# Lightning attention and a tanh-shrink MLP on one core: one quarter-product of the first matmul moved to a second Strassen level

## The chip, the cores and the metric

The kernel runs on 1 core of one Trainium2 chip. The metric is the device time in microseconds (us) of one execution; lower is better. Beside it stands one profiled execution, from which all rows below come.

## The reference, cut to what matters

```python
# q, k, v: (4, 8, 768, 64) float32; lam: (8,); w_in: (512, 2048); w_out: (2048, 512)
# attention with decay, in blocks of 64 tokens; kv_state is carried from block to block
for b in range(nb):
    intra = einsum('bhic,bhjc->bhij', qb, kb) * Dmask      # lam ** (i - j), lower triangle
    out   = einsum('bhij,bhjd->bhid', intra, vb) + einsum('bhid,bhde->bhie', qb * lam_pow, kv_state)
    kv_state = lam_block * kv_state + einsum('bhsd,bhse->bhde', kb * rev_pow, vb)
x = out.transpose(0, 2, 1, 3).reshape(3072, 512)           # tokens x (heads * head_dim)
h = x @ w_in                                               # first product:  3072 x 512 x 2048
g = h - tanh(h)
return g @ w_out                                           # second product: 3072 x 2048 x 512
```

## The kernel before

Tokens are worked in 6 groups `g` of 512 (128 positions of each of the 4 batches; `NG = 6`). The hidden dimension of 2048 is cut into 4 units `u` of 512 (`NU = 4`). For each group the order is: the first product, unit by unit (`up`), then tanh and subtraction, then the second product (`down`), and between these, in small pieces, the attention of the next group (`pieces`).

Both matrix products are Strassen-Winograd products: seven quarter-products P1 to P7 in place of eight, with sums of the operands made before and sums of the results made after. From the third group on (`g >= GI`, `GI = 2`) this is done:

- **First product.** P1 and P5 are made in two levels, for all four units at once: `inner_steps` runs seven steps (`STEPS`), each of four matmuls of 128x128 by 128 columns, one for each unit. Their token sums come from `inner_tokens` at the end of the group before, their weight sums from `inner_weights` in the second group, which also sends three of them to DRAM (`fine_in`). The steps 5, 6 and 3 read such a weight sum back as a piece. P2, P6, P7, P3 and P4 are made in one level by `up(g, u, n)`: four matmuls of 128x128 by 256 columns. `later_units` writes their order out.
- **How a unit is put together.** P1's result lies in the buffer S1 of `hidden`, P5's in buffer 22. `seeded` copies them on ScalarE into a bank of PSUM ahead of a product, which then adds to them: P2 to P1 in bank w; P6, P7 and P4 to P1 in bank ya or yb (even or odd unit); P3 to P5 in bank z. `finish` makes tanh on ScalarE (line 651) and the subtraction on VectorE (line 656). The 12 quarter is what stands after P6 (copied on ScalarE, line 662) plus bank z after P3 (VectorE, line 674). The 22 quarter adds P7 on VectorE (line 665). The 21 quarter is read straight from the bank after P4. `up_sums` (lines 698, 699) makes two operand sums of the second product on VectorE.
- **Second product.** `down_twice` makes its quarter-products in two levels: seven steps of four matmuls (line 935) in the order 1, 2, 6, 5, 7, 3, 4. Steps 1, 6, 7 and 4 add up in one bank, and ScalarE copies what stands there after each (line 938). Each operand has three sums on VectorE (`sums_twice`, line 893) and one between steps 2 and 3. The factors are pieces of 256 KB that GpSimd's queue brings from DRAM into a ring of 7 tiles (`piece`, `RING`); the order is that of `pieces_of`. `PLACES` names the PSUM banks.
- **The cover.** In the last unit, `later_units` makes the sums of the second product's P4 on VectorE and puts the attention piece "P2" of the next group (`att_both`: lines 511, 497, 461, 525 on TensorE; then two copies on ScalarE, line 415), or in the last group `down(g, 1)`, ahead of `up(g, 3, 4)`. Then the second product starts with its P4.

Each engine runs its instructions in the order in which they are recorded. PSUM has eight banks: ya, yb, z and w once each, and four under the name att.

Of the kernel before, what the change touches and what calls it, by code (L numbers as in the profile page):

```python
# [16 lines left out]
AL = mybir.AluOpType  # L17
# [7 lines left out]
def kernel(  # L25
# [188 lines left out]
    SLOT = (1, 2, 3, 6, 5, 7, 4)  # L214
    fine = dram.tile([len(TWICE), len(SUB), 128, NU, 128], F32, name="fine")

    fine_in = dram.tile([2, 3, 128, NU, 128], F32, name="fine_in")
# [409 lines left out]
    def up(g, u, n, wait=False, inside=False):  # L627
# [21 lines left out]
        def finish(c, src):  # L649
            th = work.tile([128, 2, HB], F32, name="th", tag="th")  # L650
            tied(g == 0, nc.scalar.activation(th, src, AF.Tanh))  # L651
            if g >= GI:
                pieces(g, ("t", u, c))
                if (u, c) in ((2, 12), (3, 12), (3, 22)):
                    next(made[g, 2], None)
            tied(g == 0 or g >= GI and inside, nc.vector.tensor_tensor(dst(c), src, th, op=AL.subtract))  # L656

        if g >= GI:
            if n == 2:
                finish(11, t)  # L660
            elif n == 6:
                nc.scalar.activation(dst(12), t, AF.Copy)
            elif n == 7:
                def end():
                    tied(inside, nc.vector.tensor_tensor(dst(22), dst(22), t, op=AL.add))
                    finish(22, dst(22))

                if wait:
                    return end
                end()  # L670
            elif n == 4:
                finish(21, t)
            else:
                tied(inside, nc.vector.tensor_tensor(dst(12), dst(12), t, op=AL.add))  # L674
                finish(12, dst(12))
            return
# [24 lines left out]
    INNER = (1, 5)  # L701
    toks = {}

    def a_quarter(n, u, i, k):
        return w1[u][:, k, 0, ts(i, 128)] if n == 1 else ws[u][:, 0, k, ts(i, 128)]

    def inner_weights(u, ns=INNER):
        for n in ns:
            a11, a12, a21, a22 = (a_quarter(n, u, i, k) for i in range(2) for k in range(2))
            t = late["pool"].tile([128, 4, 128], F32, name="ws2", tag="sums", bufs=4)  # L710
# [4 lines left out]
            nc.gpsimd.dma_start(out=fine_in[INNER.index(n)].rearrange("x p u c -> p u x c")[:, u], in_=t[:, 0:3])  # L715

    def inner_tokens(g):
        for n in INNER:
            x = xt[g][FACT[n][1]]
            b11, b12, b21, b22 = (x[:, k, ts(j, 128)] for k in range(2) for j in range(2))  # L720
            t = late["pool"].tile([128, 4, 128], F32, name="tt2", tag="sums", bufs=4)
            t1, t2, t4 = (t[:, x] for x in range(3))
            for dst, x, y in ((t1, b12, b11), (t2, b22, t1), (b12, b22, b12), (t4, b21, t2)):
                nc.vector.tensor_tensor(dst, x, y, op=AL.subtract)
            toks[g, n] = {1: b11, 2: b21, 3: b22, 4: t4, 5: t1, 6: t2, 7: b12}

    STEPS = (1, 5, 2, 6, 7, 3, 4)

    def inner_steps(g, n, tag):

# [1 line left out]
        out4 = hidden(g, "S1" if n == 1 else 22)  # L732
        c11, c12, c21, c22 = (out4[:, :, i, ts(j, 128)] for i in range(2) for j in range(2))
        for x in STEPS:
            b = toks[g, n][x]
            wb = piece(g, ("in", n), x) if x in (3, 5, 6) else None
            dst = w if x == 2 else z if x in (3, 5) else y
            for u in range(NU):
                a = wb.rearrange("p m c -> p (m c)")[:, ts(u, 128)] if wb is not None else a_quarter(
                    n, u, *{1: (0, 0), 2: (0, 1), 7: (1, 0), 4: (1, 1)}[x])  # L740
                tied(True, nc.tensor.matmul(out=dst[:, ts(u, 128)], lhsT=a, rhs=b, start=x in (1, 2, 5) and u == 0,  # L741
                                            stop=True, skip_group_check=True))
# [29 lines left out]

    def pieces_of(g):
        if g >= GI:
            yield from ((g, ("in", 5), x) for x in STEPS if x in (5, 6, 3))
        for n in order(g):
            yield from ((g, n, x) for x in (SUB if twice(g, n) else range(NU)))
        if g == NG - 1:
# [125 lines left out]
    def sum_third(g, n):  # L904
# [5 lines left out]

    PLACES = {GI - 1: {4: ("w", "yb"), 5: ("att", "w"), 6: ("yb", "z"), 7: ("w", "att"), 3: ("z", "att")},
              NG - 1: {4: ("att", "att"), 7: ("att", "yb"), 5: ("att", "w"), 2: ("yb", "ya"), 6: ("w", "att")}}
    PLACES.update({g: {4: ("att", "att"), 7: ("att", "yb"), 5: ("att", "w"), 1: ("yb", "z"), 2: ("w", "ya"),
                       6: ("z", "att"), 3: ("ya", "att")} for g in range(GI, NG - 1)})

    def down_twice(g, n):
        a11, a12, a21, a22 = quarter(g, n)
        s1, s2 = low.pop((g, n))
        places = PLACES[g][n]
        begins = (1, 2) if places[0] == "att" or (g, n) == (GI - 1, 4) else (2,)  # L920
# [301 lines left out]
    def second_units(g):  # L1222
        for u in range(NU):
            for n in (2, 6, 5, 7, 1, 4, 3):
                if n != 1:
                    up(g, u, n)
                elif u + 1 < NU:
                    up(g, u + 1, 1)
                else:
                    pieces(g, u)  # L1230
                    inner_weights(u, INNER[:1])
                    every(down(g, 1))
                if u < 2 and n == 5:
                    sums_in(u + 2)
            inner_weights(u, INNER if u + 1 < NU else INNER[1:])
            if u + 1 < NU:
                pieces(g, u)

    def later_units(g):
        for n in (1, 2):  # L1240
            made[g, n] = fine_factors(n) if g == GI else iter(())
        for u in range(NU):
            if u < 2:
                next(made[g, u + 1], None)
            for n in ("next", 3, "S", 4) if u == 0 else (6, "next", 7, 3, "S", 4) if u + 1 < NU else (
                    6, 3, 7, "S", "P4", "cover", 4):
                if n == "next":
                    up(g, u + 1, 2, inside=True)
                elif n == "S":
                    up_sums(g, u)  # L1250
                elif n == "P4":
                    sums_twice(g, 4)
                elif n == "cover":
                    if twice(g, 1):
                        pieces(g, "P2")
# [4 lines left out]
            pieces(g, u)  # L1260
            if u == 0:
                every(made[g, 1])
            elif u == NU - 1:
                every(made[g, 2])

    def later_products(g):
        product = down_twice(g, 4)
# [35 lines left out]
    for g in range(1, NG):  # L1303
# [6 lines left out]
        if g == NG - 1:  # L1310
            down_end(g)
            continue
        inner_tokens(g + 1)
# [48 lines left out]
```

## Time and profile before

| what | value |
|---|---|
| median of 3 runs | 653.57 us (650.77 to 654.89) |
| profiled execution | 653.5 us, of which the span from first to last instruction is 651.7 us |
| granted TensorE clock, mean | 0.997 |
| TensorE (PE) busy | 641.0 us, 98% of the span, 5792 matmuls |
| VectorE (DVE) busy | 495.3 us, 76%, 884 instructions |
| ScalarE (ACT) busy | 241.2 us, 37%, 484 instructions |
| GpSimd (POOL) busy | 231.1 us, 35%, 396 instructions |
| DMA | 140.45 MB, mean 216 GB/s |

PE, DVE, ACT and POOL are the engines; PEld is the weight load of TensorE, which overlaps PE. L935 is line 935 of the kernel before. An entry such as `y<-wb,g` gives output and inputs by the program's names. The timeline gives start, duration, engine, line, operation, tiles and shape; what stands in square brackets is the idle time of the engine just before it and what ended that. The ends of matmuls are modelled, so rows of PE overlap a little: the distance of two starts is the better measure.

### The profile page before, as it was taken

The page shows a single profiled execution, that of the slowest core. Times are in us where ns is not written, and L with a number is a line of the kernel's source. Part 1 is how long each engine was busy: PE and PEld are TensorE (multiplying, and loading weights), DVE is VectorE, ACT ScalarE, POOL GpSimd, SP SyncE. Part 2 cuts the span into 40 slices and gives each one's busy share as a digit, 9 for nine tenths or more (in the row PEclk, how much of TensorE's full clock was granted, in tenths as well). Part 3 has the DMA queues.
Part 4 walks back from the last instruction along what each step waited for, and adds up shares of the span by engine and source line. Part 5 has one row for each costly group of instructions (what it writes and reads, how often), then busy time and mean ns, then how long its engine had stood idle before and what let it go on. Part 6 is the DMA issues. An engine that isn't in the chain of part 4 may idle for free.

```text
span 651.7 us, 14766 instructions
## 1 busy us (share of the span) xinstructions
PE 641.0 (98%) x5792; PEld 590.9 (91%) x5792; DVE 495.3 (76%) x884; ACT 241.2 (37%) x484; POOL 231.1 (35%) x396
## 2 busy tenths in 40 slices
PE   8999999999999999999999999999999999999998
PEld 6788888888888999888999988999988999988997
DVE  4897988987877967888868777878777878256583
ACT  3878683513322124442122453122344212444110
POOL 2210248783113554233455100546201456300450
PEclk9999999999999999999899999999999999999999
DMA  9879979999468877999878766778693587610482
GB/s 215 248 196 215 253 243 296 323 324 279 127 160 220 265 238 220 246 284 250 268 238 295 197 140 129 246 238 310 194 188 98 164 289 253 209 41 0 156 289 74
DMA packets 108197, 140.45 MB, mean 216 GB/s; under 512 B 63968, under 2 KB 81504, under 8 KB 108128
## 3 DMA queue, kind: packets, MB, share of 16 engines
q0 software_dynamic: 29840, 97.54, 46.8%
q1 hardware_dynamic: 78144, 41.96, 27.2%
q8 instruction: 46, 0.75, 0.5%
q14 instruction: 23, 0.19, 0.1%
q10 hardware_dynamic: 144, 0.00, 0.0%
HBM read 117.18 MB, written 23.86 MB: 216 GB/s over the span
## 4 chain that ended last, share of the span: by engine, by line
PE 86%; issue 5%; DMA 3%; POOL 2%; DVE 2%; ACT 1%; SPq 1%; POOLq 0%; DVEq 0%; ACTq 0%
PE y L935 16%; PE y L643 15%; PE zw L935 12%; PE acc L1045 7%; PE h L1015 6%; PE z L643 6%; PE w L643 5%; PE y L741 4%; PE z L741 2%; PE y L870 2%; DMA wb<-fine 2%; PE sp L461 2%; PE op L511 2%; PE op L497 1%; PE kv L424 1%
## 5 line engine op out<-in xcount | busy, mean ns | idle before, releaser
L817 POOL DMA_DIRECT2D wb<-fine x217 | 116.8, 539 | 220.5 <-PE y L935 112.5
L935 PE MATMUL y<-wb,g 128*128 128x128 f32 x624 | 81.3, 276 | 0.2 <-DMA wb<-fine 0.2
L938 ACT ACTIVATE q<-y 128x128 f32<-128x128 f32 x108 | 30.0, 278 | 138.4 <-PE y L935 138.4
L935 PEld LDWEIGHTS y<-wb,g 128*128 128x128 f32 x624 | 75.3, 192 | 1.1 <-issue 0.6
L935 PE MATMUL zw<-wb,g 128*128 128x128 f32 x416 | 55.2, 276 | 0.7 <-DMA wb<-fine 0.6
L935 PEld LDWEIGHTS zw<-wb,g 128*128 128x128 f32 x416 | 50.6, 192 | 1.2 <-PE y L935 0.8
L643 PE MATMUL y<-xt,w 128*128 128x256 f32 x200 | 46.9, 380 | 0.0
L651 ACT ACTIVATE th<-g 128x512 f32<-128x512 f32 x42 | 26.5, 631 | 51.9 <-DVE g L674 20.3
L1015 PE MATMUL h<-xt,w 128*128 128x256 f32 x192 | 44.2, 382 | 1.4 <-DVE w L325 1.4
L656 DVE TENSOR_TENSOR g<-g,th 128x512 f32<-128x512 f32 x42 | 29.2, 694 | 17.4 <-ACT th L651 17.2
L643 PEld LDWEIGHTS y<-xt,w 128*128 128x128 f32 x200 | 37.6, 190 | 5.1 <-ACT g L683 0.2
L1015 PEld LDWEIGHTS h<-xt,w 128*128 128x128 f32 x192 | 35.7, 190 | 6.8 <-DVE w L325 1.3
L643 PE MATMUL w<-xt,w 128*128 128x256 f32 x168 | 40.4, 382 | 0.0
L643 PE MATMUL z<-xt,ws 128*128 128x256 f32 x168 | 39.7, 379 | 0.0
L643 PE MATMUL y<-tt,w 128*128 128x256 f32 x160 | 38.1, 381 | 0.0
L643 PE MATMUL y<-tt,ws 128*128 128x256 f32 x160 | 38.1, 380 | 0.0
L643 PEld LDWEIGHTS z<-xt,ws 128*128 128x128 f32 x168 | 31.9, 190 | 4.3
L935 PE MATMUL y<-wb,s 128*128 128x128 f32 x248 | 33.8, 281 | 1.5 <-DMA wb<-fine 1.4
L643 PEld LDWEIGHTS w<-xt,w 128*128 128x128 f32 x168 | 31.0, 190 | 4.5 <-ACT w L614 0.4
L643 PEld LDWEIGHTS y<-tt,w 128*128 128x128 f32 x160 | 30.1, 190 | 4.2
L643 PEld LDWEIGHTS y<-tt,ws 128*128 128x128 f32 x160 | 30.0, 190 | 3.9
L935 PE MATMUL zw<-wb,s 128*128 128x128 f32 x248 | 33.5, 279 | 0.0
(216 smaller groups left out, 1376.2 us busy)
## 6 DMA issues: line engine op xcount, KB each, us to landing
wb<-fine POOLq DMA_DIRECT2D x217, 256.0 KB, 3.9
raw<-in_moe_w_in_dram SPq DMA_DIRECT2D x12, 512.0 KB, 5.2
fine<-f POOLq DMA_DIRECT2D x24, 256.0 KB, 4.8
wb<-fine_in POOLq DMA_DIRECT2D x24, 256.0 KB, 4.2
raw<-in_moe_w_out_dram POOLq DMA_DIRECT2D x10, 512.0 KB, 6.3
q_blk<-in_q_dram SPq DMA_DIRECT2D x32, 128.0 KB, 4.4
k_blk<-in_k_dram SPq DMA_DIRECT2D x32, 128.0 KB, 5.1
wb<-factors POOLq DMA_DIRECT2D x16, 256.0 KB, 4.5
```

The source lines that it names most:

```text
L461: tied(True, nc.tensor.matmul(out=dst, lhsT=keys(p, j, late_), rhs=qt[ts(j, 64), p, rows], start=True, stop=True))
L511: tied(True, nc.tensor.matmul(out=dst(n, p, j)[:, HF:BLK], lhsT=vn[:, 2 * p + j, :], rhs=ss[:, j, p % 2, 1 + p // 2, :], start=first and n ...
L643: tied(g == 0, nc.tensor.matmul(out=t[:, m, :], lhsT=wt[:, kt, ts(m, 128)], rhs=x[:, kt, :], start=first and m == 0 and kt == 0, stop=kt = ...
L651: tied(g == 0, nc.scalar.activation(th, src, AF.Tanh))
L656: tied(g == 0 or g >= GI and inside, nc.vector.tensor_tensor(dst(c), src, th, op=AL.subtract))
L741: tied(True, nc.tensor.matmul(out=dst[:, ts(u, 128)], lhsT=a, rhs=b, start=x in (1, 2, 5) and u == 0, stop=True, skip_group_check=True))
L817: nc.gpsimd.dma_start(out=t.rearrange("p m c -> p (m c)"), in_=fine[TWICE.index(n_), SLOT.index(x_)].rearrange("p u c -> p (u c)"))
L870: nc.tensor.matmul(out=t[:, m, :], lhsT=a[:, u, kt, ts(m, 128)], rhs=wb[:, kt, :], start=first and u == 0 and m == 0 and kt == 0, stop=u = ...
L935: tied(True, nc.tensor.matmul(out=dst, lhsT=a[:, u, :], rhs=wb[:, ts(u, 128)], start=x in begins and u == 0, stop=u == NU - 1, skip_group_ ...
L938: nc.scalar.activation(keep, dst, AF.Copy)
L1015: tied(u == 0 or u == 2 and cs[0] == 11, nc.tensor.matmul(out=hm[c][:, m, :], lhsT=w1[u][:, i, a, ts(m, 128)], rhs=xt[0, t][:, i, :], star ...
L1045: nc.tensor.matmul(out=acc[n][:, r, :], lhsT=a[:, ts(r, 128)], rhs=b, start=kt == 0 and r == 0, stop=kt == KH - 1, skip_group_check=True)
```

## The change

From the third group on, P4 of the first product is made in two levels for all units at once, as P1 and P5 are:

- `up(g, u, 4)` is gone from `later_units`. After P7 of each unit, ScalarE copies the bank (P6+P7 on top of P1) into buffer 21.
- `inner_last` ("U4") comes after the last unit's `up_sums` and ahead of the sums of the second product's P4: seven steps of four matmuls of 128 columns, in the order 1, 5, 6, 2, 7, 3, 4, in the banks ya, w, z and one of att. Three of their results are copied on ScalarE (two of them into other banks, to be added to), four are added to buffer 21 on VectorE.
- `finish_last` comes behind the sums of the second product's P4: one addition of 128x1024 to buffer 21, then four times tanh and subtraction.
- The token sums (`inner_tokens(g, 4)`) are taken one by one at the 11 quarter of the units 1 to 3. The weight sums are made in the second group, in tiles of their own, and go to DRAM on ScalarE's queue. Each group has three more pieces in the ring, between those of P5 and those of the second product.
- The second product's P4 moves to the banks z and yb, its P7 to two banks of att. In the third group the last factor sums (`made[g, 2]`) end ahead of "U4" and no longer behind the last unit.

```diff
     def finish(c, src):
             ...
             if g >= GI:
                 pieces(g, ("t", u, c))
                 ...
+                if c == 11 and u:
+                    steps(made[g, "T4"], 1 + u // 3)
...
             elif n == 7:
                 def end():
+                    nc.scalar.activation(dst(21), t, AF.Copy)
                     tied(inside, nc.vector.tensor_tensor(dst(22), dst(22), t, op=AL.add))
                     finish(22, dst(22))
...
+    LAST = (1, 5, 6, 2, 7, 3, 4)
+    def inner_last(g):
+        y, w, z5, z3 = bank("y3", "ya", 1), bank("w3", "w", 1), bank("z5", "att", 4), bank("z3", "z", 1)
+        r5 = otile("r5")
+        out4 = hidden(g, 21)
+        c11, c12, c21, c22 = (out4[:, :, i, ts(j, 128)] for i in range(2) for j in range(2))
+        for x in LAST:
+            dst = {2: w, 3: z3, 5: z5}.get(x, y)
+            inner_matmuls(g, 4, x, dst, x in (1, 5))
+            if x in (1, 6):
+                nc.scalar.activation(w if x == 1 else z3, y, AF.Copy)
+            elif x == 5:
+                nc.scalar.activation(r5, z5, AF.Copy)
+            else:
+                c = {2: c11, 7: c22, 3: c12, 4: c21}[x]
+                hold(c, c, dst.rearrange("q (u c) -> q u c", u=NU), op=AL.add)
+        return r5
+    def finish_last(g, r5):
+        c = hidden(g, 21)
+        cols = c[:, :, :, ts(1, 128)]
+        hold(cols, cols, r5.rearrange("q (u c) -> q u c", u=NU)[:, :, None, :].to_broadcast([128, NU, 2, 128]), op=AL.add)
+        for u in range(NU):
+            th = work.tile([128, 2, HB], F32, name="th", tag="th")
+            nc.scalar.activation(th, c[:, u], AF.Tanh)
+            hold(c[:, u], c[:, u], th, op=AL.subtract)
...
         if g >= GI:
-            yield from ((g, ("in", 5), x) for x in STEPS if x in (5, 6, 3))
+            yield from ((g, ("in", n), x) for n in (5, 4) for x in STEPS if x in (5, 6, 3))
...
-    PLACES.update({g: {4: ("att", "att"), 7: ("att", "yb"), 5: ("att", "w"), 1: ("yb", "z"), 2: ("w", "ya"),
+    PLACES.update({g: {4: ("z", "yb"), 7: ("att", "att"), 5: ("att", "w"), 1: ("yb", "z"), 2: ("w", "ya"),
...
     def second_units(g):
                     inner_weights(u, INNER[:1])
+                    for v in range(u):
+                        inner_weights(v, INNER[2:])
                     every(down(g, 1))
...
     def later_units(g):
+        made[g, "T4"] = inner_tokens(g, 4)
         for u in range(NU):
             ...
-            for n in ("next", 3, "S", 4) if u == 0 else (6, "next", 7, 3, "S", 4) if u + 1 < NU else (
-                    6, 3, 7, "S", "P4", "cover", 4):
+            for n in ("next", 3, "S") if u == 0 else (6, "next", 7, 3, "S") if u + 1 < NU else (
+                    6, 3, 7, "S", "U4", "P4", "cover"):
                 ...
                 elif n == "S":
                     up_sums(g, u)
+                    if u + 1 == NU:
+                        every(made[g, 2])
+                elif n == "U4":
+                    r5 = inner_last(g)
                 elif n == "P4":
                     sums_twice(g, 4)
+                    finish_last(g, r5)
```

More of the change, by code (lines that the diff above doesn't have):

```diff
@@ L215 @@
     fine = dram.tile([len(TWICE), len(SUB), 128, NU, 128], F32, name="fine")
-    fine_in = dram.tile([2, 3, 128, NU, 128], F32, name="fine_in")
+    fine_in = dram.tile([3, 3, 128, NU, 128], F32, name="fine_in")
     w_in_u = moe_w_in.rearrange("k (u a n) -> k u a n", u=NU, a=2)
@@ L699, in up_sums, with inner_weights @@
         tied(g >= GI, nc.vector.tensor_tensor(c12, c11, c12, op=AL.subtract))
-    INNER = (1, 5)
+    INNER = (1, 5, 4)
     toks = {}
     def a_quarter(n, u, i, k):
-        return w1[u][:, k, 0, ts(i, 128)] if n == 1 else ws[u][:, 0, k, ts(i, 128)]
-    def inner_weights(u, ns=INNER):
+        return (w1[u][:, k, 0] if n == 1 else ws[u][:, 0, k] if n == 5 else w1[u][:, 2 + k, 1])[:, ts(i, 128)]
+    def inner_weights(u, ns=INNER[:2]):
         for n in ns:
             a11, a12, a21, a22 = (a_quarter(n, u, i, k) for i in range(2) for k in range(2))
-            t = late["pool"].tile([128, 4, 128], F32, name="ws2", tag="sums", bufs=4)
+            t = otile("ws4").rearrange("p (x c) -> p x c", x=4) if n == 4 else late["pool"].tile(
+                [128, 4, 128], F32, name="ws2", tag="sums", bufs=4)
             s1, s2, s4 = (t[:, x] for x in range(3))
@@ L714, in inner_weights @@
                 tc.keep_in_program_order(nc.vector.tensor_tensor(dst, x, y, op=op))
[L715 to L725, printed above, removed]
@@ L727, with inner_tokens @@
-    STEPS = (1, 5, 2, 6, 7, 3, 4)
+            eng = nc.scalar if n == 4 else nc.gpsimd
+            eng.dma_start(out=fine_in[INNER.index(n)].rearrange("x p u c -> p u x c")[:, u], in_=t[:, 0:3])
+    def inner_tokens(g, n):
+        x = xt[g][FACT[n][1]]
+        b11, b12, b21, b22 = (x[:, k, ts(j, 128)] for k in range(2) for j in range(2))
+        t = otile("tt4").rearrange("p (x c) -> p x c", x=4) if n == 4 else late["pool"].tile(
+            [128, 4, 128], F32, name="tt2", tag="sums", bufs=4)
+        t1, t2, t4 = (t[:, x] for x in range(3))
+        toks[g, n] = {1: b11, 2: b21, 3: b22, 4: t4, 5: t1, 6: t2, 7: b12}
+        for dst, x, y in ((t1, b12, b11), (t2, b22, t1), (b12, b22, b12), (t4, b21, t2)):
+            tied(n == 4, nc.vector.tensor_tensor(dst, x, y, op=AL.subtract))
+            yield
@@ new lines, with inner_matmuls @@
+    STEPS = (1, 5, 2, 6, 7, 3, 4)
+    def inner_matmuls(g, n, x, dst, begin):
+        b = toks[g, n][x]
+        wb = piece(g, ("in", n), x) if x in (3, 5, 6) else None
+        for u in range(NU):
+            a = wb.rearrange("p m c -> p (m c)")[:, ts(u, 128)] if wb is not None else a_quarter(
+                n, u, *{1: (0, 0), 2: (0, 1), 7: (1, 0), 4: (1, 1)}[x])
+            tied(True, nc.tensor.matmul(out=dst[:, ts(u, 128)], lhsT=a, rhs=b, start=begin and u == 0,
+                                        stop=True, skip_group_check=True))
@@ L729, in inner_steps @@
+    def finish_last(g, r5):
+        c = hidden(g, 21)
+        cols = c[:, :, :, ts(1, 128)]
+        hold(cols, cols, r5.rearrange("q (u c) -> q u c", u=NU)[:, :, None, :].to_broadcast([128, NU, 2, 128]), op=AL.add)
+        for u in range(NU):
+            th = work.tile([128, 2, HB], F32, name="th", tag="th")
+            nc.scalar.activation(th, c[:, u], AF.Tanh)
+            hold(c[:, u], c[:, u], th, op=AL.subtract)
     def inner_steps(g, n, tag):
@@ L734, in inner_steps @@
         for x in STEPS:
-            b = toks[g, n][x]
-            wb = piece(g, ("in", n), x) if x in (3, 5, 6) else None
             dst = w if x == 2 else z if x in (3, 5) else y
[L738 to L742, printed above, removed]
+            inner_matmuls(g, n, x, dst, x in (1, 2, 5))
             d = dst.rearrange("q (u c) -> q u c", u=NU)
@@ L919, in down_twice @@
         places = PLACES[g][n]
-        begins = (1, 2) if places[0] == "att" or (g, n) == (GI - 1, 4) else (2,)
+        begins = (1, 2) if places[0] == "att" or n == 4 else (2,)
         y, zw = (bank(name, t, 4 if t == "att" else 1) for name, t in zip(("y2", "zw"), places))
@@ L1234, in second_units @@
                     sums_in(u + 2)
-            inner_weights(u, INNER if u + 1 < NU else INNER[1:])
+            inner_weights(u, INNER[:2] if u + 1 < NU else INNER[1:])
             if u + 1 < NU:
@@ L1262, in later_units @@
                 every(made[g, 1])
-            elif u == NU - 1:
-                every(made[g, 2])
     def later_products(g):
@@ L1312 @@
             continue
-        inner_tokens(g + 1)
+        for n in INNER[:2]:
+            every(inner_tokens(g + 1, n))
         p3 = down_twice(g, 3)
```

## The prediction

> I call the groups g0 to g5 and the units u0 to u3; the change acts in g2 to g5 and, for the weight sums, in g1.
>
> **What bounds the kernel now.** I read the page first: TensorE is busy nearly throughout.
>
> ```profile
> span 651.7 us, 14766 instructions
> ...
> PE 641.0 (98%) x5792; PEld 590.9 (91%) x5792; DVE 495.3 (76%) x884; ACT 241.2 (37%) x484; POOL 231.1 (35%) x396
> ```
>
> Then the waits of TensorE alone. In the changed groups it waits only for pieces in g2, some 2.2 us with the next line of this kind; for VectorE or ScalarE it doesn't wait there at all.
>
> ```profile
> PE y L935 <- DMA wb<-fine: 1.6, 2, 1.4
> ```
>
> Then busy time by stretches: the units of g3 (373 to 410) and its second product (410 to 456). PE fills both to the last tenth; VectorE has 9 us of idle time in the first.
>
> ```profile
> 373.00:410.00 37.00, 37.00 (x335) 33.00 (x332) 28.15 (x42) 16.24 (x30) 1.07 (x2) 1.00 0.62 132
> 410.00:456.00 46.00, 45.94 (x479) 45.24 (x478) 38.22 (x73) 9.73 (x31) 26.84 (x49) 1.00 0.82 277
> ```
>
> So a shorter TensorE sequence shortens the time only while nobody makes TensorE wait. The chain that ended last prices a matmul (x16 is 8 matmuls and 8 weight loads): 3.45/8 = 0.432 us with 256 columns, 1.79/8 = 0.224 us with 128.
>
> ```profile
> 394.18 3.45 PE y L643 x16
> ...
> 412.38 1.79 PE y L935 x16
> ```
>
> Last, the timeline of g3 in two places. First, from P3 of u2 to P3 of u3:
>
> ```profile
> 392.29 1.89 PE L643 MATMUL z<-xt,ws 128*128 128x256 f32 x8
> 392.49 0.69 DVE L665 TENSOR_TENSOR g<-g,y 128x512 f32<-128x512 f32 x1 [0.25 <-PE y L643]
> 393.10 1.15 DVE L354 STREAM_TRANSPOSE kt<-k_blk 128x512 f32<-128x512 f32 x1
> ...
> 394.06 0.71 DVE L656 TENSOR_TENSOR g<-g,th 128x512 f32<-128x512 f32 x1
> 394.66 0.70 DVE L674 TENSOR_TENSOR g<-g,z 128x512 f32<-128x512 f32 x1
> 395.45 0.63 ACT L651 ACTIVATE th<-g 128x512 f32<-128x512 f32 x1 [1.55 <-DVE g L674]
> 395.99 0.58 ACT L619 ACTIVATE z<-g 128x512 f32<-128x512 f32 x1
> ...
> 397.47 1.89 PE L643 MATMUL z<-xt,ws 128*128 128x256 f32 x8
> ```
>
> Bank z is read by L674, refilled by L619, and only then may P3 of u3 start; between the two P3 TensorE has P4 of u2 and P6 of u3. Second, from the cover to the first steps of the second product:
>
> ```profile
> 401.02 1.15 PE L511 MATMUL op<-ss,v_nat 128*64 128x64 f32 x32
> 405.03 1.99 PE L643 MATMUL y<-tt,w 128*128 128x256 f32 x8
> 405.04 1.08 ACT L415 ACTIVATE xt<-op 128x512 f32<-128x512 f32 x2 [1.60 <-PE op L525]
> 406.86 1.05 PE L935 MATMUL y<-wb,g 128*128 128x128 f32 x8
> 407.95 0.28 ACT L938 ACTIVATE q<-y 128x128 f32<-128x128 f32 x1 [0.23 <-PE y L935]
> 408.65 1.06 PE L935 MATMUL y<-wb,s 128*128 128x128 f32 x8
> ```
>
> The third row's two copies and the fifth row's copy are ScalarE's; the last row (step 6) adds to the bank that the fifth row copied, so it must come behind it.
>
> **The change, part by part.** I follow the order of the changed program's instructions on each engine and put the durations of these rows to it.
>
> *A, matmuls.* Per group 16 x 0.432 = 6.91 us go, 28 x 0.224 = 6.26 come: -0.65, four groups -2.6. The first product's own steps stand at 0.89 to 0.95 us for four, so the bounds are -2.8 and -1.0.
>
> *B, P3 of u3 late.* Without P4 of u2, TensorE is at P3 of u3 1.73 us sooner after P3 of u2. In the rows above the bank was full at 396.57 and the weight load began at 397.26, so 0.7 was spare: short by 1.0. ScalarE now copies the ya or yb bank into buffer 21 after P7, and in the built program the addition of line 665 waits for that copy (0.6), with the whole chain behind it: subtraction, L674, tanh, refill. Short by 1.6. VectorE also loses cover before that: P4 of u0 and u1 took 3.45 us of TensorE, but only 1.4 us of subtractions. Counting its 16 operations at their distance of 0.60 to 0.73 and four transposes at 0.96 from 376.25 on, with the waits for ScalarE, the refill ends at 393.8 where TensorE arrives at 392.2: 1.7 in g3 and g4. In g5, without transposes, the chain alone gives 1.6. In g2 four more subtractions (L893, 2.86 us from 274.34) lie before it, partly in waits: I take 3.0. Sum 8.0; bounds 4.0 (1.0 each, if copy and addition could overlap) and 11.
>
> The Trainium skill ("PSUM — Partial Sum Buffer", section "PSUM bank collisions raise a hardware error") says that two engines, readers too, must not be in the same bank and quadrant at once, and that a dependency is put between them. By that rule the copy and line 665 run one after the other, as I have it; without it the sum would be 2.2 lower, 665.3. No row of before has two readers of one bank side by side, so this trace doesn't show it.
>
> *C, waits inside the new product.* Step 7 waits for a ScalarE copy of the same bank, step 4 for VectorE's addition of step 7. VectorE has still to do line 698 and 699 of u3, then the additions of the steps 2 and 7: in g3 these end 0.25 us after TensorE has come to step 4, and 0.1 goes at step 7. Taken: 0.4, 0.4, 0.5 and 0.4, sum 1.7; bounds 0 and 3.2.
>
> *D, step 6 of the second product's P4 late.* From the last matmul of "U4": 0.3 to its result; addition and three sums of P4, 2.55; the addition of 128x1024, 1.2 (line 839's rows); tanh 0.65, subtraction 0.7, and as `th` has two tiles the third tanh waits for the first subtraction and the fourth for the second, 1.25 more: 6.65. On ScalarE, behind these four tanh, stand the two copies of line 415 (1.1) and then the copy that step 6 waits for (0.3): 8.05. TensorE's cover is the attention piece (401.02 to 405.03, 4.0) and the steps 1 and 2 (1.8): 5.8. It waits 2.3 in each of g2, g3, g4: 6.9. In g5 the cover is `down(g, 1)` with 6.9, and line 415 isn't there: 0. Bounds per group 1.8 (every operation at its shortest distance) and 3.0: 5.4 and 9. Nothing later suffers: the fourth sum that step 3 needs comes 1.6 after step 6 has begun, step 3 2.7 after it.
>
> The Trainium skill ("TensorE: Matmul & The Clock Gate", section "Architectural detail: the array is 16× 32×32, not 1× 128×128") says that ScalarE's and VectorE's queues are strictly first in, first out, while TensorE may pull weight loads forward. If a ready copy could pass a waiting tanh, this term would be gone and the sum would give 660.6. The trace agrees with the rule: the refill at 395.99 needed only bank z, free at 395.36, and stood behind the tanh of 395.45.
>
> *E, what is hidden.* The 16 operations for the weight sums of g1 (0.20 apart at line 714: 3.2 us) lie beside `down(1, 1)` (6.9 us), their four DMAs on ScalarE's queue too; without that cover 2 us: bounds 0 and 2. VectorE's twelve small token sums are in B. Three more pieces a group: they take ring places that the second product's P4 had from early on, so its last three pieces are issued during "U4"; the first of them is needed more than 9 us after its issue against a landing of 3.9. In g2 the 2.2 us of waits for pieces may shrink, as TensorE comes later, or grow as GpSimd's queue holds two factor stores behind those pieces: 0, bounds -2.2 and +2. The new banks of P4 and P7 are free before they are wanted (z after the addition of step 3, the att banks after line 415).
>
> **Sum:** -2.6 + 8.0 + 1.7 + 6.9 + 0 = +14.0, against the profiled 653.5 (span 651.7 and 1.8 around it; the median is 0.07 above): **667.5 us**. By group: g2 5.2, g3 and g4 3.7, g5 1.4.
>
> **Rivals.**
> - *Everything hidden.* If the waits of B to D fall into slack that I don't see, A remains: 650.9; with the waits for pieces gone too, 648.7. For it speaks only that 24% of VectorE's and 63% of ScalarE's span is idle; against it, that the waits come from order and not from load. This is the case that ends on the other side. It decides from the point at which bank z is refilled by 392.2 in g3, that is 1.0 sooner after P7 than the rows allow.
> - *Only one of the two waits.* B without C and D: 653.5 - 2.6 + 8.0 = 658.9. D and C without B: 659.5. B is the surer one: it rests on a measured slack of 0.7 against 1.73.
> - *The backlog spreads.* In the second product VectorE is busy for 38.2 of 46 us. If it stays 1 us behind, a step of the next two products waits in g2 to g4 also: 3 x 2 = 6 more, 673.5. Against it: in D TensorE waits longer than VectorE is late.
>
> **Chances.** The forecast 0.64, one wait alone 0.18, all hidden 0.09, spread 0.09. 1% (6.5 us, to 660.1) is about what a measurement of this kernel can tell from no change. Slower by over 1%: nearly all of the forecast, the spread, and a third of the one-wait case (with its terms at their upper bounds): 0.77. Within 1%: the rest, 0.21; faster by over 1% would need more than A and the pieces give: 0.02. All lower bounds together give 658, all upper ones 680. Range 655 to 674: out of it lie the hidden case and the tail of the spread.
>
> **What would show it.** Right: TensorE idle of 1.5 to 3 us ahead of `z<-xt,ws` of u3 once in each of g2 to g5, released by ScalarE (the refill); 2 to 3 us ahead of the third step of the second product's first quarter-product in g2 to g4 and none in g5, released by ScalarE line 976; "U4" at 6.3 to 7 us from first to last step. Wrong: TensorE at 98% or more in these stretches, "U4" much above 7, or waits for `wb` in their place.

## The result, and the profile after

The changed kernel takes 673.78 us (median of 6 runs), the kernel before 653.24 us beside it: ratio 1.0319, 95% interval 1.0290 to 1.0347, so it is slower by 3.2%. The forecast was 667.5 with a range of 655 to 674. The direction was right, the size 6.3 us too small, and the largest single loss lies in a group to which the prediction gave nothing.

The page of the changed kernel, its span and its busy time by engine:

```profile
span 672.0 us, 15039 instructions
...
PE 643.3 (96%) x5888; PEld 591.9 (88%) x5888; DVE 517.0 (77%) x936; ACT 255.3 (38%) x512; POOL 238.1 (35%) x408
```

The profile counts two matmuls for each of the program's, so the 48 more of the change are 96 here. They come to much the same PE time, but PE falls from 98% of the span to 96%. VectorE's and ScalarE's shares grew by one point each; the time went into waits. They are in the list of TensorE's waits (who waits, for whom, us in total, times, the longest):

```profile
PE z L643 <- ACT z L619: 4.2, 4, 1.3
PE y L973 <- ACT q L976: 3.0, 3, 1.8
PE zw L973 <- DVE s L931: 2.1, 1, 2.1
PE y L643 <- ACT g L664: 1.7, 4, 0.7
...
PE y L741 <- DVE g L931: 1.4, 1, 1.4
...
PE zw L973 <- DVE g L931: 1.3, 1, 1.3
PE zw L973 <- issue: 1.3, 1, 1.3
...
PE op L525 <- ACT probe L501: 1.0, 1, 1.0
PE y L908 <- DVE g L931: 0.8, 1, 0.8
```

The first line is term B (P3 of u3 waits until ScalarE has refilled z), the second term D, the fifth term C. The third, sixth and eighth lie in g1; the seventh lies in g2. Only waits of TensorE above 0.2 us are listed, so the sum is a lower bound.

To see where the 20.3 us of longer span arose, I set TensorE's groups of instructions in the two traces side by side and took the growth of the difference of their starts (a group ends here where the units of the next begin):

| group | predicted | measured |
|---|---|---|
| g1 | 0 | 6.8 |
| g2 | 5.2 | 0.9 |
| g3 | 3.7 | 5.4 |
| g4 | 3.7 | 4.0 |
| g5 | 1.4 | 2.8 |

**g1.** The timeline of VectorE in the changed kernel, at the end of the transposes, at the last weight sums and at the first sum for the second product:

```profile
202.97 1.12 DVE L354 STREAM_TRANSPOSE kt<-k_blk 128x512 f32<-128x512 f32 x1
203.92 0.30 DVE L718 TENSOR_TENSOR ws<-w 128x128 f32<-128x128 f32 x1
...
209.11 0.29 DVE L718 TENSOR_TENSOR ws<-w 128x128 f32<-128x128 f32 x1 [1.08 <-DMA fine_in<-ws]
...
210.05 0.68 DVE L931 TENSOR_TENSOR s<-g 128x512 f32<-128x512 f32 x1
```

and the last two rows of the same place in the kernel before:

```profile
205.19 0.29 DVE L714 TENSOR_TENSOR ws<-ws,ws 128x128 f32<-128x128 f32 x1
205.39 0.69 DVE L893 TENSOR_TENSOR s<-g 128x512 f32<-128x512 f32 x1
```

Between 203.9 and 210.0 VectorE does 24 weight sums in place of 8, with a wait of 1.08 us for a transfer that must free a tile. `down(1, 1)` runs on TensorE from 199.26 to 206.3, so two thirds of it are over when the first sum starts. The sums for the second product start 4.66 us later. The next stretches by engine (PE, PEld, DVE, ACT, POOL, clock, DMA share, GB/s), first before, then after:

```profile
211.00:217.00 6.00, 6.00 (x56) 6.00 (x56) 5.97 (x10) 1.35 (x5) 3.41 (x7) 1.00 0.70 207
217.00:223.00 6.00, 6.00 (x57) 6.00 (x56) 5.83 (x11) 0.97 (x4) 3.63 (x7) 1.00 0.89 291
```

```profile
211.00:217.00 6.00, 5.15 (x72) 4.89 (x65) 5.41 (x8) 1.92 (x5) 2.74 (x5) 1.00 1.02 289
217.00:223.00 6.00, 5.53 (x48) 5.43 (x48) 5.89 (x10) 0.83 (x3) 2.66 (x5) 1.00 1.05 255
```

VectorE was already full here, at 5.97 and 5.83 of 6 us. It had nothing with which to catch up, and what was put ahead of it came out at the end.

**g3, the two waits that were foreseen.** Timeline of the changed kernel: the copy of bank ya into 21 after P7 of u2, the addition that waits for it, the refill of z, P3 of u3:

```profile
397.59 0.60 ACT L667 ACTIVATE g<-y 128x512 f32<-128x512 f32 x1 [1.59 <-PE y L643]
398.22 0.69 DVE L668 TENSOR_TENSOR g<-g,y 128x512 f32<-128x512 f32 x1 [0.45 <-ACT g L667]
...
401.69 0.58 ACT L619 ACTIVATE z<-g 128x512 f32<-128x512 f32 x1
402.32 1.99 PE L643 MATMUL z<-xt,ws 128*128 128x256 f32 x8 [1.31 <-ACT z L619]
```

and then ScalarE at the start of the second product, with step 6 of its P4:

```profile
416.55 1.15 ACT L770 ACTIVATE th<-g 128x512 f32<-128x512 f32 x2 [1.52 <-DVE g L931]
417.94 1.23 ACT L770 ACTIVATE th<-g 128x512 f32<-128x512 f32 x2 [0.24 <-DVE g L931]
419.08 1.07 ACT L415 ACTIVATE xt<-op 128x512 f32<-128x512 f32 x2
420.03 0.28 ACT L976 ACTIVATE q<-y 128x128 f32<-128x128 f32 x1
420.36 1.16 PE L973 MATMUL y<-wb,s 128*128 128x128 f32 x8 [1.79 <-ACT q L976]
```

Both are the chains that the prediction drew: four Tanh, two copies, then the copy of step 1, and step 6 right behind it.

### The profile page after: what moved, and what is told of

Same layout as the page of the kernel before. It is cut to its first block, busy times and chain, and to the rows that moved or that the text cites. A ratio compares the mean times of both kernels' runs of the same rounds, so it can differ in the third digit from the quotient of the medians.

```text
span 672.0 us, 15039 instructions
## 1 busy us (share of the span) xinstructions
PE 643.3 (96%) x5888; PEld 591.9 (88%) x5888; DVE 517.0 (77%) x936; ACT 255.3 (38%) x512; POOL 238.1 (35%) x408
## 4 chain that ended last, share of the span: by engine, by line
PE 68%; issue 11%; DVE 8%; DMA 6%; ACT 4%; POOL 2%; SPq 1%; DVEq 0%; POOLq 0%; ACTq 0%
PE y L973 14%; PE zw L973 11%; PE acc L1083 7%; PE y L643 7%; PE h L1053 6%; PE y L741 5%; PE z L643 3%; PE z L741 2%; DMA q_blk<-in_q_dram 2%; PE w L643 2%; PE y L908 2%; POOL wb L855 1%; DVE g L931 1%; PE w L741 1%; SPq L156 1%
## 5 line engine op out<-in xcount | busy, mean ns | idle before, releaser
L973 PEld LDWEIGHTS y<-wb,s 128*128 128x128 f32 x248 | 30.2, 192 | 4.1 <-ACT q L976 3.6
L931 DVE TENSOR_TENSOR g<-g,s 128x512 f32<-128x512 f32 x26 | 17.9, 688 | 16.3 <-PE zw L973 16.2
```

Of the source, the lines that this page charges most:

```text
L931: tc.keep_in_program_order(nc.vector.tensor_tensor(*args, **kw))
L973: tied(True, nc.tensor.matmul(out=dst, lhsT=a[:, u, :], rhs=wb[:, ts(u, 128)], start=x in begins and u == 0, stop=u == NU - 1, skip_group_ ...
```

## The experiments

Times are medians; each is compared by its ratio to the kernel before, measured beside it. For the changed kernel that ratio is 1.0319. A difference between two single traces says less: at the end of g1 the traces of two kernels that are the same as the changed one up to there lie 2.1 us ahead of its trace and 1.4 behind it.

### The weight sums of g1: four runs

My theory after the result: the 16 extra sums delay VectorE's queue. Rivals: the transfers, which hold ScalarE's queue; or the pieces and the longer ring.

**The sums alone, in the kernel before**

```diff
+    def more_weights(u):                # the same four sums as for n == 4, not in place
+        ...
+        nc.scalar.dma_start(out=fine_in[2].rearrange("x p u c -> p u x c")[:, u], in_=t[:, 0:3])
                     inner_weights(u, INNER[:1])
+                    for v in range(u):
+                        more_weights(v)
                     every(down(g, 1))
             inner_weights(u, INNER if u + 1 < NU else INNER[1:])
+            if u + 1 == NU:
+                more_weights(u)
```

> The kernel before, with P4's weight sums of g1 alone added: the same 16 VectorE operations of 128x128 at the same place in VectorE's queue as in the changed kernel and the same four transfers on ScalarE's queue. The sums are not used by anything. Nothing else of the change is in it. Theory 1, that these alone made g1 6.8 us longer: 659 to 661 against 653. The prediction's term E, that they lie beside down(1,1): 653 to 655. If it comes between, at 656 or 657, the place in the queue is part of the cause and the rest belongs to what the change does with the pieces.

Measured: 660.87 us, ratio 1.0123 (1.0088 to 1.0158), 8.1 us over the kernel before. This trace is 1.1 us late before the sums begin; up to 227 us the difference grows to 6.1, so g1 itself loses 5.0. VectorE's rows are those of the changed kernel: 24 weight sums with a wait for a transfer, then the first sum of the second product, at 210.84.

```profile
209.90 0.29 DVE L723 TENSOR_TENSOR ws<-w 128x128 f32<-128x128 f32 x1 [0.93 <-DMA fine_in<-ws]
...
210.84 0.69 DVE L902 TENSOR_TENSOR s<-g 128x512 f32<-128x512 f32 x1
```

In g2 the difference first falls by 2.3 (6.73 at 306.5 to 4.44 at 314.3) and rises again by 3.8 up to 350.8; its largest waits are now for pieces.

```profile
PE zw L944 <- DMA wb<-fine: 4.2, 3, 2.3
```

Sixteen operations that nothing uses, 3.2 us of VectorE, cost 8 us with their four transfers: some 5 in g1, the rest behind it. Term E stands disproved without any other part of the change.

**Transfers on another queue**

```diff
-            eng = nc.scalar if n == 4 else nc.gpsimd
+            eng = nc.sync if n == 4 else nc.gpsimd
```

> The changed kernel, but the four transfers of P4's weight sums of g1 are issued from SP's queue instead of ScalarE's, where they stood at 206 to 208 us and waited for VectorE's sums with the copy of down(1,1) and the probe behind them. If that hold of ScalarE's queue is what costs g1 its 6 to 7 us: g1 loses 1 to 3 us instead, and the time falls by 4 to 6, to about 669. If VectorE's queue is what costs (the second product's sums start 4.7 us late behind the 16 operations): g1 keeps at least 5 us of its loss and the time stays at 672 to 675.

Measured: 674.15 us, ratio 1.0317 (1.0287 to 1.0347): no change. ScalarE is free, its copy of `down(1, 1)` no longer stands behind the transfers, and yet the sum `s` starts at 210.28:

```profile
206.25 0.60 ACT L921 ACTIVATE o<-w 128x512 f32<-128x512 f32 x1 [5.54 <-PE w L908]
...
209.34 0.29 DVE L718 TENSOR_TENSOR ws<-w 128x128 f32<-128x128 f32 x1 [1.49 <-DMA fine_in<-ws]
...
210.28 0.69 DVE L931 TENSOR_TENSOR s<-g 128x512 f32<-128x512 f32 x1
```

TensorE's wait for ScalarE's `probe` is gone, and at 211 us this trace is 1.4 ahead; but the two waits for VectorE's sums are there as before (3.3 us together), with more waits for pieces. So ScalarE's queue is not what sets the loss, though the trace had named `probe` as what TensorE waited for.

**The sums moved behind the second product**

```diff
-            t = otile("ws4").rearrange("p (x c) -> p x c", x=4) if n == 4 else late["pool"].tile(
+            t = work.tile([128, 4, 128], F32, name="ws4", tag="th") if n == 4 else late["pool"].tile(
     ...
-                    for v in range(u):
-                        inner_weights(v, INNER[2:])
-            inner_weights(u, INNER[:2] if u + 1 < NU else INNER[1:])
+            inner_weights(u, INNER[:2] if u + 1 < NU else INNER[1:2])
     ...                                  # in the in-turn loop at the end of the group, n = its step
+            if g < GI and n in (3, 5, 7, 9):
+                inner_weights((n - 3) // 2, INNER[2:])
```

> The changed kernel, but P4's weight sums of g1 (16 VectorE operations and four transfers) leave the units of g1 and are issued one unit at a time among the in-turn steps at the end of g1. Theory 1, that g1 lost its 6.8 us because these 16 operations stand in VectorE's queue just ahead of the second product's sums, where VectorE was already busy 5.2 to 6.0 us of every 6: g1 loses under 1 us against the kernel before and the time falls by 6 to 7, to about 667. Theory 2, that the loss comes from the third tile of pieces in memory and from the longer ring of pieces (the transfers, not the place of the sums): g1 keeps its loss wherever the sums stand, and the time stays at 672 to 675. Between them, if the sums cost the same behind the end of g1, the loss moves from the window of 204 to 224 us to the in-turn stretch and the time is about 670.

Measured: 669.81 us, ratio 1.0265 (1.0225 to 1.0305). By 230 us the trace has gained 6.7 on the changed kernel, nearly all that g1 had lost; by 315 us 4 of them are gone again. Of these, 1.7 are lost at the steps of the in-turn stretch (the end of a group, where steps of the second product alternate with the first ones of the next group), which now wait for VectorE and ScalarE there, and 2.4 at the start of the second product of g2:

```profile
PE zw L973 <- issue: 2.7, 1, 2.7
...
PE y L741 <- DVE gS L931: 0.7, 1, 0.7
PE y L741 <- ACT q L976: 0.5, 1, 0.5
```

So g1 loses its time by the place of the sums, not by the pieces; but this later place gives part of it back. Why is not shown in full. VectorE is busy for 7.3 of the 10 us from 250 to 260, so it isn't full there. The sums also lie in tiles of tanh's name (`th`) in this run. What ends the wait of 2.7 us the profile doesn't say.

**The sums on GpSimd**

```diff
-                tc.keep_in_program_order(nc.vector.tensor_tensor(dst, x, y, op=op))
-            eng = nc.scalar if n == 4 else nc.gpsimd
+                tc.keep_in_program_order((nc.gpsimd if n == 4 else nc.vector).tensor_tensor(dst, x, y, op=op))
+            eng = nc.gpsimd
     ...                                  # in second_units: at the end of each unit
-                    for v in range(u):
-                        inner_weights(v, INNER[2:])
     ...
+            inner_weights(u, INNER[2:])
```

> The changed kernel, but P4's weight sums of g1 run on GpSimd, at the end of each unit, with their transfers on GpSimd's queue; in the trace of after GpSimd is at 2 to 3 tenths there. By the three 128x512 subtractions that GpSimd does in g0 (1.4 to 1.7 us each) 16 of a quarter of that width take 6 to 10 us in all, spread over 65 us. Theory 1, that VectorE's queue at 204 to 224 us is the whole of g1's loss: g1's loss falls from 6.8 to under 1.5 and the time to 667 to 669; as nothing is put later in exchange, it gains more than the sums moved into the in-turn stretch (which kept about 4 of its 5.5 us). Rival: the two engines slow each other down or the last unit's sums now hold GpSimd's queue with the pieces of the second product behind them (four operations of about 0.5 us and a transfer at about 205 us): then waits for pieces of 2 us or more show up at 210 to 224 us and the time stays above 670.

Measured: 665.99 us, ratio 1.0194 (1.0168 to 1.0220), the lowest of any single edit of the changed kernel. Stretch 211 to 217: PE is full but for 0.09 us, with GpSimd at 5.51 of 6.

```profile
211.00:217.00 6.00, 5.91 (x53) 5.71 (x52) 5.97 (x10) 1.47 (x6) 5.51 (x9) 1.00 0.57 158
```

By 230 us it has gained 6.6 on the changed kernel; 0.8 of this is lost again at 247, and by the end it is 7.1 ahead. Against the kernel before, g1 still loses 1.2. The waits of g2 to g5 are all still there. The edit changes two things, the engine and the place: the sums of u0 to u2 also leave the crowded end of g1 for the ends of their own units. Whether VectorE could have done them there was not run; in the kernel before it is busy for only 4.29 of the 10 us from 190 to 200.

### Term B: three runs

**u3's z in a bank of its own**

```diff
-        t = banks["up", g, u, x] = bank(x, {"y": ("ya", "yb")[u % 2]}.get(x, x), 1)
+        if x == "z" and u == NU - 1:
+            t = banks["up", g, u, x] = bank(x, "att", 4)
+        else: ...
```

> The changed kernel, but the z bank of unit u3 alone is taken from the att banks instead of z, so that P3 of u3 has not to wait until ScalarE has refilled z. Theory 1, that term B (P3 of u3 late, about 1.5 us of waits in each of g3, g4 and g5 by the trace of after) is a wait that ends when the bank is free: the group of waits PE z on ACT z shrinks from 4.2 us to about 0.3 and the time falls by 3.5 to 5.5, to 668 to 670. Theory 2, that the wait covers other work of ScalarE and VectorE that is needed a little later (the copies into 12 and 22 and their sums, the inner steps): the waits turn up again behind it, at P7 of u3, at step 6 or 4 of the new product or at step 6 of the second product's P4, and the time falls by less than 1.5, to 672 or more.

Measured: 668.30 us, ratio 1.0252 (1.0209 to 1.0296). This kernel doesn't begin the att bank as z is begun, and its quarter 12 of u3 is not the sum that it should be; the instructions are those of the changed kernel. The group of waits for z is gone. In its trace 2.1 us of the gain lie ahead of g2, where the edit changes nothing. In g2 most of the rest comes back: P3 of u3 starts 2.8 us sooner, of which 1.3 are only that P7 now follows it whole; 1.6 are left at step 1 of the new product and 0.4 at its step 6.

**u3's z in ya, the banks of the new product exchanged**

```diff
+        tag = "ya" if x == "z" and u == NU - 1 else {"y": ("ya", "yb")[u % 2]}.get(x, x)
+        t = banks["up", g, u, x] = bank(x, tag, 1)
-        y, w, z5, z3 = bank("y3", "ya", 1), ..., bank("z3", "z", 1)
+        y, w, z5, z3 = bank("y3", "z", 1), ..., bank("z3", "ya", 1)
```

> The changed kernel, but u3's z stands in bank ya (free since u2's P7) and the new product uses the two banks the other way round: its y in z, its step 3 in ya. All instructions stay. It does what the run with u3's z in an att bank did (which lost the waits of P3 of u3 and gave 0.5 to 1.2 us of them back at steps 6 and 4 of the new product in g2), and it also frees ya earlier for down(5,1) in g5 (0.8 us of wait there in after). Theory 1 (term B is a wait for a bank): 668 to 669.5, the group PE z on ACT z gone and at most half of it found again behind it. Theory 2 (the wait only moves, since ScalarE and VectorE are late by the same amount behind it): 672 or more.

Measured: 669.49 us, ratio 1.0237 (1.0201 to 1.0274). What the waits of TensorE show in place of 4.2 (z) and 1.4 (step 4):

```profile
PE y L742 <- DVE g L932: 2.5, 4, 1.4
...
PE z L644 <- ACT z L620: 0.4, 1, 0.4
```

By step 1 of the new product, 1.0 us is gained in g2, 1.6 in g3 and g4 and 1.4 in g5. Its later steps take 0.7 back in g3 and g4, and in g2 step 6 and the second product take back all of it. `down(5, 1)` no longer waits in g5. Theory 1 for g3 to g5, theory 2 for g2.

**The addition ahead of the copy**

```diff
-                    nc.scalar.activation(dst(21), t, AF.Copy)
                     tied(inside, nc.vector.tensor_tensor(dst(22), dst(22), t, op=AL.add))
+                    nc.scalar.activation(dst(21), t, AF.Copy)
```

> The changed kernel, but VectorE's addition of P7 into 22 is recorded ahead of ScalarE's copy of the same bank into 21, so the pair that the trace of after shows one behind the other (copy 0.60 us, then the addition 0.45) runs in the other order. Theory 1, that the additions of 22 are late by the copy and that this lateness is what reaches P3 of u3 (term B): the additions and with them the sums and the refill of z come 0.6 us earlier, the waits of P3 of u3 shrink by about that in each of four groups, and the time falls by 1.5 to 2.5, to about 672. Theory 2, that the refill of z hangs on ScalarE's queue and not on the addition: the copy now waits for the addition and holds ScalarE's queue for 0.5 us longer, the waits of P3 of u3 stay or grow by some tenths, and the time is 673 to 676.

Measured: 676.00 us, ratio 1.0349 (1.0321 to 1.0377). That is 2 us the other way, but the interval overlaps that of the changed kernel, and 1.3 us of it arise in this trace ahead of g2, where the edit changes nothing. The pair still runs one behind the other, and ScalarE now stands waiting (timeline of VectorE and ScalarE in g3):

```profile
392.40 0.69 DVE L667 TENSOR_TENSOR g<-g,y 128x512 f32<-128x512 f32 x1 [0.35 <-PE y L643]
393.12 0.60 ACT L668 ACTIVATE g<-y 128x512 f32<-128x512 f32 x1 [0.43 <-DVE g L667]
```

Behind it in ScalarE's queue stand the copies that P7 waits for, and in the list of waits P7 now waits up to 1.1 us for its copy, where 0.7 was the most:

```profile
PE y L741 <- DVE g L931: 3.0, 4, 1.4
...
PE z L643 <- ACT z L619: 2.4, 2, 1.2
...
PE y L643 <- ACT g L664: 1.8, 2, 1.1
```

In g3 and g4 the wait at P3 of u3 falls only from 1.3 to 1.2, as theory 2 has it. P7's wait of 0.3 is gone there, and step 4 of the new product waits 0.3 instead. In g2 and g5 the wait moves from P3 to P7 and to the new product's steps. So the order of the pair isn't the cure. That the pair itself is what costs is likely, but no run without it shows that.

### Term D: one run

```diff
+        yield
         for u in range(NU):
             th = work.tile([128, 2, HB], F32, name="th", tag="th")
-            nc.scalar.activation(th, c[:, u], AF.Tanh)
+            tied(True, nc.scalar.activation(th, c[:, u], AF.Tanh))
             hold(c[:, u], c[:, u], th, op=AL.subtract)
+            yield
     ...                                  # in later_products; the copies of line 976 are tied too
-        steps(product, 4)
+        for _ in range(4):
+            next(product)
+            next(made[g, "fin"])
```

> The changed kernel, but the four Tanh and subtractions that end the new product are issued two by two behind the first copy of the second product's P4 instead of all four ahead of it; the copies and Tanh keep that order on ScalarE. Theory 1, that term D (step 6 of that product waits for a copy that stands behind four Tanh) is right: the waits of step 6 (3.0 us in three, and 1.3 us of issue in g2) go to under 1 us together, and the time falls by 2.5 to 4.5, to about 670. Theory 2, that step 6 waits for something else that is late too (the sums on VectorE, the pieces): the wait at step 6 stays within 0.5 us of what it was or comes back at step 7 or 4, and the time stays within 1.5 of 673.8. A third outcome is that the subtractions now come late for the next sums of the hidden quarter 22 and the third product waits: then the time grows.

Measured: 669.44 us, ratio 1.0260 (1.0226 to 1.0294). In g3 the copy that step 6 needs now stands ahead of the Tanh, and step 6 starts without a wait:

```profile
419.60 0.28 ACT L978 ACTIVATE q<-y 128x128 f32<-128x128 f32 x1
419.77 1.14 ACT L771 ACTIVATE th<-g 128x512 f32<-128x512 f32 x2
...
420.29 1.06 PE L975 MATMUL y<-wb,s 128*128 128x128 f32 x8
```

Against the changed kernel the trace gains 2.1 at this place in g3 and another 1.0 at a wait for a piece 10 us later, and 1.1 at this place in g4 with 0.7 just ahead of the product. Theory 1 for these two. In g2 it gains 0.5 at this place and loses 1.1 to a wait for a piece behind it: there TensorE idles in the middle of step 2, and that stays.

```profile
314.49 0.49 PE L975 MATMUL zw<-wb,g 128*128 128x128 f32 x3 [1.40 <-issue]
```

What ends this wait the profile doesn't show, and no run settled it.

### The gains together: two runs

**GpSimd sums, exchanged banks, Tanh in steps**

The edits are the diffs of the three runs above.

> The changed kernel with the three edits together that gained alone: P4's weight sums of g1 on GpSimd (alone 665.99, so 7.8 less than 673.8), u3's z in ya with the banks of the new product exchanged (alone 669.49, 4.3 less), and the Tanh and subtractions of the new product two by two behind copies of the second product's P4 (alone 669.44, 4.4 less). If the three causes are separate waits that lie one behind another, the gains add: 657 to 658. If the later ones feed on the same backlog of VectorE and ScalarE, part of the gains is shared or returns as waits at the new product's steps 4 and 6: 659 to 663. In the first case the rest above the kernel before is 4 to 5 us, in waits of P7 for the copy into 12 (0.3 to 0.7 each), of step 4 (1.4 in g2) and on pieces.

Measured (5 rounds): 659.52 us, ratio 1.0087 (1.0073 to 1.0101). The three gains add to 16.5 us and give 14.3, the second of the two cases expected. By groups the loss against the kernel before is now 0.6 in g1, 0.3 in g2, 2.3 in g3, 2.0 in g4, 0.8 in g5. Ahead of the new product 0.6 to 0.7 a group remain at P7. The new product takes 8.8, 7.5, 7.4 and 7.2 us. In g3 these are its second and third step (5 and 6), its last (4), and the attention piece that follows:

```profile
398.31 1.06 PE L742 MATMUL z<-tt,wb 128*128 128x128 f32 x8
399.42 1.16 PE L742 MATMUL y<-tt,wb 128*128 128x128 f32 x8
...
403.80 1.16 PE L742 MATMUL y<-tt,w 128*128 128x128 f32 x8 [0.35 <-DVE g L934]
404.89 1.15 PE L511 MATMUL op<-ss,v_nat 128*64 128x64 f32 x32
```

From its first step (397.42) to 404.89 it takes 7.47 us. Seven steps at 0.89 are 6.26, and the four P4 that it replaces took 6.91. Term A's saving of 0.65 a group is thus spent inside the product itself: steps 6, 2, 7 and 3 start 0.99 to 1.11 us after the one before in place of 0.89, and step 4 1.40.

**Step 4 in a bank of its own as well**

```diff
-            dst = {2: w, 3: z3, 5: z5}.get(x, y)
-            inner_matmuls(g, 4, x, dst, x in (1, 5))
+            dst = {2: w, 3: z3, 5: z5}.get(x, y) if x != 4 else bank("z4", "att", 4)
+            inner_matmuls(g, 4, x, dst, x in (1, 5, 4))
```

> The three edits and one more: step 4 of the new product writes a bank of its own (att) instead of the bank of steps 1, 6 and 7, so that it need not wait for VectorE's addition of step 7 (1.4 us in g2, 0.3 to 0.4 in g3 to g5 in the trace with the exchanged banks). If that wait sets the end there: 2 to 2.5 us below the run with three edits, about 655; term A (2.6 us of matmuls saved) would then still be eaten by the remaining waits. If the next user of the sums (the second product's steps or the Tanh) waits as long behind it: within 1 us of the run with three. Should all the waits go, term A alone would remain and it would be 651; that is not expected, since the additions of 22 are still one copy late and the pieces of g2 run without the slack that they had in the run of after.

Measured (5 rounds): 658.75 us, ratio 1.0067 (1.0049 to 1.0085). This kernel leaves out the sum of steps 1, 6 and 7 from quarter 21, so it only shows what the wait of step 4 costs. The new product now takes 7.1, 6.8, 6.8 and 6.8 us in the four groups, in place of 8.8, 7.5, 7.4 and 7.2, but only 0.8 us reach the end, within the intervals of the two: a wait for pieces takes the room in g2.

```profile
PE zw L976 <- DMA wb<-fine: 2.2, 1, 2.2
```

None of the changed versions here is faster than the kernel before.

## Why the prediction was right and where it was wrong

By the starts of TensorE's instructions, the 20.3 us of longer span come from these places, set against the terms of the prediction (0.2 lie elsewhere):

| term | predicted | measured |
|---|---|---|
| A and C, the new product in place of P4 | -2.6 and +1.7 | -2.6 and +4.4 |
| B, up to the new product | 8.0 | 8.0 |
| D, up to step 6 of the second product's P4 | 6.9 | 6.2 |
| E, sums of g1 | 0 | 6.8 |
| E, pieces of g2 | 0 | -4.3 |
| later in the second product of g3 | 0 | 1.6 |

- **E is the step that failed.** The prediction laid the weight sums of g1 beside `down(1, 1)` at no cost, with 2 us as the bound if that cover were gone. Three runs set 4 to 8 us against this: alone the sums cost 8, moved to GpSimd they give back 7.8, moved behind the second product 4.0. The cover was TensorE's, and VectorE came to the sums only at 203.9, when it had done the sums and transposes ahead of them; two thirds of `down(1, 1)` were over. What lay behind them was a VectorE that was busy for 97% of the time and more. The prediction read VectorE's idle share in the units of g3 and in the second product, never in g1 where the sums run. Its bound of 2 us is below the 3.2 us that it gives for the operations themselves, and it counted neither the wait for a tile nor the lack of later slack.
- **E's other half, the pieces of g2, hid the size of this.** The 2.2 us of waits for pieces went, as the lower bound allowed, and with slower steps around them 4.5 us came back between 306 and 315 us. The run with the sums alone shows the same in part (2.3). So g2 looks cheap in the table by groups, with 0.9 against 5.2; its own waits were there. Both halves lie outside their bounds on opposite sides, so that the total missed by only 6.3 is in part luck.
- **B was right in kind and in sum, not in its parts.** Idle time at P3 of u3 was there in all four groups, released by ScalarE's refill: 4.2 us in the list. Another 1.7 stood at P7 for a copy that the prediction hadn't listed. By the starts, which also count what the list leaves out, g2 loses 1.6, g3 and g4 2.2 each and g5 2.0, against 3.0, 1.7, 1.7 and 1.6. That these add to the same 8.0 is luck: g2 was too dear by as much as the missing P7 made the others too cheap. Another bank took the wait at P3 away (one of the two runs kept 0.4 in g2), and left 1.0 of that at P7.
- **The rule of the Trainium skill in B held.** Copy 21 and the addition run one behind the other in both orders (398.19 to 398.22, 393.09 to 393.12), as the Trainium skill's page "PSUM — Partial Sum Buffer" ("PSUM bank collisions raise a hardware error") has it. The sum without that rule, 2.2 lower, would have been the worse one.
- **D was right in place, chain and releaser in g3 and g4.** By the list step 6 waited 1.8 in g3 (2.3 foreseen) and 0.9 in g4, in g5 not at all, as forecast. In g4 another 0.8 lies ahead of the product, in the attention piece. In g2 the 2.1 us at this place are mostly another wait, which stayed when the Tanh moved; that the number fits there is luck. The strict order of ScalarE's queue (the Trainium skill, "TensorE: Matmul & The Clock Gate", "Architectural detail: the array is 16× 32×32, not 1× 128×128") shows in g3: the copy of step 1 started at 420.03, behind two copies for the next group, while the result lay there since 417.7.
- **C was too small.** From first to last step and on to what follows, the new product takes 8.48, 6.72, 6.72 and 7.57 us: 2.2, 0.5, 0.5 and 1.3 above 6.26, which is 4.4 against 1.7 and above the bound of 3.2. In g2 step 4 waits 1.4 for the addition, in g5 `down(5, 1)` waits 0.8 for bank ya. "U4" much above 7 was named as a sign of being wrong, and g2 and g5 show it.
- **The rivals.** "The backlog spreads" gave 673.5 and a chance of 0.09; its number fits, its mechanism hardly: behind g3's first quarter-product the second product lost 1.6 us more, in g4 nothing to speak of, and in g2 it gained. That everything is hidden is refuted, and so is that one of the two waits comes alone. In the combined runs A's saving is still spent in and around the new product.
- **Small slips that change nothing.** By the prediction's own terms g2 comes to 5.05 and g4 to 3.85, not 5.2 and 3.7; the total stays 14.0. A refill at 393.8 against an arrival at 392.2 makes 1.6, not 1.7. The x16 of the chain are 16 matmuls as the profile counts them, two for each of the program's eight, and no weight loads are among them; the price of 0.432 us for each of the eight holds.

## What to carry to other kernels

Before work is called hidden, read the busy share of the engine that does it in the stretch where it will really run, and in the one after: behind a queue that is 97% full there is no slack, and 3.2 us put into it cost 5 to 8. Then look for an engine with room, or for a stretch in which the same engine idles: here GpSimd gave back 7.8 us and a later place on VectorE 4.0, and an earlier place on VectorE remains to be tried. A product cut into shorter steps needs its copies and additions done within a step: here, where four of seven steps share one accumulating bank, the 9% less matmul time was spent on waits between them.

## What the runs showed of the hardware

GpSimd and VectorE were slower where both worked on tiles in SBUF at once. GpSimd's 128x128 operations of line 718 took 0.45 us at the least and up to 1.44 while VectorE was full (by the starts of the rows too, 1.40); VectorE's 128x512 took up to 0.94 in place of 0.69 in the same stretch. Two rows of the run with the sums on GpSimd:

```profile
209.53 1.44 POOL L718 TENSOR_TENSOR w<-w 128x128 f32<-128x128 f32 x1
210.58 0.94 DVE L931 TENSOR_TENSOR s<-gS 128x512 f32<-128x512 f32 x1
```

The Trainium skill ("SBUF — State Buffer", "SBUF: two separate sides") says that the two share a pair of ports, which one of them holds for a whole instruction. The longer rows (1.44 and 0.94 us) fit that; who held the ports they don't show. It was no obstacle here: GpSimd had the time, and with the sums there g1 lost 1.2 us in place of 6.8.
